# Pooling the first two batches' keys and values on TensorE, with the first weights loaded and decoded ahead of the values

## The chip, the cores and the metric

The kernel runs on one core of a Trainium2 chip. The metric is the time of one execution on the device in microseconds (us), the median over several runs; smaller is better.

## The reference, cut to what matters

Three stages follow each other: attention over pooled keys and values, a dense layer pair with `h * cos(h)` between, and a mixture of eight experts of which each token takes one. The inputs are 8 batches of 8 heads, 576 positions and 64 dimensions, all float32. Only the first stage is touched by the change:

```python
pool = 8
k_p = k.reshape(B, H, Sp, pool, D).mean(axis=3)      # 576 positions -> 72
v_p = v.reshape(B, H, Sp, pool, D).mean(axis=3)
scores = scale * np.matmul(q, k_p.transpose(0, 1, 3, 2))
scores = scores - np.max(scores, axis=-1, keepdims=True)
attn = np.exp(scores)
attn = attn / (np.sum(attn, axis=-1, keepdims=True) + 1e-09)
out = np.matmul(attn, v_p)
# x: 4608 tokens of 512 values
h = x @ w_in;  x = (h * np.cos(h)) @ w_out           # 512 -> 2048 -> 512
```

Each mean is over eight neighbouring positions of one batch; the kernel takes sums and puts the factors 1/8 elsewhere (into the scale of the exponential and into the division of the rows).

## The kernel before, in words

The 4608 tokens are worked in 12 groups (`g`) of 384, and each group in 16 steps (`s`), one for each 128 of the 2048 hidden columns. Step `s` runs `mm1(s)` on TensorE (12 matmuls, L394), `chain_a(s)` and `chain_b(s)` on ScalarE, VectorE and GpSimd (the cosine, L402 to L413), and `mm2(s - 2)` on TensorE (9 matmuls, L420). The attention of group `g + 1` is threaded through the steps of group `g`: `scores` (L335 to L350), `norm` (L355 to L358), `transp` (L365 to L371) and `pv` (L382 to L386). After the 12 groups come the experts.

**Order of the work.** The order is written out by hand: every engine runs its own instructions in the order in which the program issues them, and waits in place when an operand isn't ready. What is issued on SyncE (SP) is DMAs; they too start in program order. A list `ex[s]` holds what is called at the end of step `s` of a group (`at(s, f, ...)` appends to it).

**The weights.** `w_in` and `w_out` lie in memory as 64-bit floats. A pair of pieces `k` (16 pairs, 1 MB each, 512 KB a piece) passes through four functions: `w_load(k)` (two DMAs, L510), `w_scale(k)` (two ScalarE instructions, L514), `w_bits(k)` (six VectorE instructions, L519 to L521; it uses two PSUM banks in between) and `w_parts(k)` (two casts on ScalarE, L526, and two subtractions on GpSimd, L527). In group 0, step `s` calls, inside `chain_a(s)`, `w_bits(s + 3)`, `w_parts(s + 2)`, `w_scale(s + 4)` and `w_load(s + 5)`; `chain_b(s - 1)` is called between the second and the third instruction of `w_bits(s + 3)`. Pairs 0 to 2 are decoded ahead of group 0 (L604 to L622). From group 1 on the weights stay on the chip.

**Pooling.** `load_k` and `load_v` (L307 to L320) bring four tiles of a batch each, 288 KB a tile, the keys as 128 x 576 and the values as 72 x 1024, so that the eight neighbours stand side by side, and `pool_k` and `pool_v` (L313, L324) sum them with one VectorE reduction a tile. Batch 0 is pooled before group 0, with its values between the scores and the first `w_bits`; the keys of batch 1 are pooled at the end of steps 0 and 1 of group 0, its values at the end of step 14. Batches 2 to 7 are pooled in later groups; the change leaves them as they are.

**PSUM banks.** `rot()` hands out banks in turn: seven of them ahead of group 0, and only two (banks 6 and 7) from L625 on. `w_bits`, `scores`, `transp` and `pv` draw from it, so an instruction that writes a bank waits until the former holder's last reader is done.

**Around the start.** After the scores of the first three token tiles, the program before issues on ScalarE in this order: the exponentials of tiles 0 and 1 (L348, eight each), the one of tile 2 (L350), `w_scale(0)`, the copies of transposed tiles 0 and 1 (L369), `w_scale(1)`, the copies of tile 2, `w_parts(0)`, and then the casts of `pv` (L385) with `w_scale(2)` and `w_parts(1)` between.

Of the kernel before, what the change touches and what calls it, by code (L numbers as in the profile page):

```python
# [19 lines left out]
B, H, S, D = 8, 8, 576, 64  # L20
KP = 72
NT = B * S
DM = 512
# [51 lines left out]
    return np.concatenate([p[:, None] < p[None, :], np.ones((128, 128))], axis=1).astype(np.float32)  # L75


@with_exitstack
def attention_moe_kernel(ctx, tc, qT, kT, vP, w_in, w_out, wg, w1, w2, cst, tri, wgt, out, dbg=None):
    nc = tc.nc  # L80
    PE, ACT, DVE, POOL, SP = nc.tensor, nc.scalar, nc.vector, nc.gpsimd, nc.sync

# [37 lines left out]
    def w_tmp(s):  # L120
        n_tmp[0] += 1
        return wbp.tile([128, 1024], F32, name=f"tmp{n_tmp[0]}", tag=f"wb{s}")
# [175 lines left out]
    def raw():  # L298
        kvb_i[0] += 1
        return kvb[kvb_i[0] % len(kvb)]  # L300
# [4 lines left out]
    kraw = {}  # L305

    def load_k(b, c):  # L307
        t = w_tmp(12 + c)[:, 0:S] if b == 0 else raw()[:, 0:S] if b == 1 else kin
        SP.dma_start(out=t, in_=kT[b, c])
        kraw[b, c] = t  # L310

# [3 lines left out]
    vraw = {}  # L315

    def load_v(b, c):
        t = w_tmp(8 + c)[0:KP] if b == 0 else raw()[0:KP]
        SP.dma_start(out=t, in_=vP[b, c])
        vraw[b, c] = t  # L320

    def pool_v(b, c):
        t = vraw.pop((b, c))
        DVE.tensor_reduce(vp[b % 2][:, 128 * c:128 * c + 128], t.rearrange("p (f j) -> p f j", j=8), axis=AX.X, op=ALU.add)  # L324

    def scores(T, i, act=False):
        t0 = i * TP
# [24 lines left out]
    def norm(i, act=False):  # L352
        att, rs = atts[i % len(atts)], rss[:, i]
        if not act:
            DVE.tensor_reduce(rs, att, axis=AX.X, op=ALU.add)  # L355
        DVE.tensor_scalar(rs, rs, 1e-9, 8.0, op0=ALU.add, op1=ALU.mult)
        DVE.reciprocal(rs, rs)
        POOL.tensor_tensor(att, att, rs.unsqueeze(2).to_broadcast([128, H, KP]), op=ALU.mult)  # L358
# [185 lines left out]
    def w_load(k):  # L544
        if k < NCH:
            o = 2 * (k % 3 if k < 11 else (k - 11) % 2)
            for p, t in zip(pairs[k], ring[o:o + 2]):
                p.load(t)

    def w_scale(k):  # L550
        if k < NCH:
            for p in pairs[k]:
                p.scale()
# [11 lines left out]
    def w_parts(k):  # L565
        if k < NCH:
            for p in pairs[k]:
                p.parts()
# [7 lines left out]
    for i in range(3):  # L576
        t = slice(i * TP, i * TP + TP)
        SP.dma_start(out=qs[:, :, t], in_=qT[:, :, t].rearrange("c p t -> p c t"))
    for c in range(4):
        load_v(0, c)  # L580
    w_load(0)
    SP.dma_start(out=E3[:, 0:256], in_=tri)
    w_load(1)
    SP.dma_start(out=tbl.rearrange("(p b r) two -> p b (r two)", p=128, b=2),
# [6 lines left out]
    us += [u[:, DM * i:DM * i + DM] for u in (u14, ldt[0]) for i in range(2)]  # L591
    w_load(2)
    scores(0, 0, True)
    pool_v(0, 0)
    scores(1, 1, True)
    norm(0, True)
    pool_v(0, 1)
    scores(2, 2)
    norm(1, True)
    norm(2)  # L600
    w_scale(0)
    pool_v(0, 2)
    pool_v(0, 3)
    w_bits(0)  # L604
    load_q(1)
    kvb[:] = [w_tmp(8 + i) for i in range(4)]
    for c in range(4):
        load_k(1, c)
    w_load(3)
    transp(0, True)  # L610
    transp(1, True)
    w_scale(1)
    transp(2, True)
    w_parts(0)
    w_bits(1)
    w_load(4)
    pv(0, 0)
# [23 lines left out]
    for g in range(NG):  # L641
# [42 lines left out]
        for b in range(1, B):  # L684
            if g == max(0, b * S // GT - 2):
                if b == 1:
                    at(11, lambda: (kvb.__setitem__(slice(0, None), ring[2:4] + ring[0:2]), kvb_i.__setitem__(0, -1)))
                for c in range(4):
                    if b == 1:
                        at(c // 2, pool_k, b, c)  # L690
                        at(11 + c // 2, load_v, b, c)
                        at(14, pool_v, b, c)
                    else:
                        at(2 + 2 * c, pool_k, b, c)
                        at(2 * c, load_k, b, c)
                if b > 1:
                    for c in range(4):
                        at((7, 10, 12, 14)[c], pool_v, b, c)
                        at((5, 7, 10, 12)[c], load_v, b, c)
# [346 lines left out]
def lay_out(inputs):  # L1046
    ca = np.ascontiguousarray

    def raw(a):
        a = ca(a)  # L1050
        return a.view(np.int64) if a.dtype == np.float64 else a

    q, k, v = inputs["q"], inputs["k"], inputs["v"]
    return {
        "qT": ca(q.transpose(1, 3, 0, 2).reshape(4, 128, NT)),
        "kT": ca(k.transpose(0, 1, 3, 2).reshape(B, 4, 128, S)),
        "vP": ca(v.reshape(B, 4, 2, KP, 8, D).transpose(0, 1, 3, 2, 5, 4).reshape(B, 4, KP, 1024)),
        "w_in": raw(inputs["moe_w_in"]),
        "w_out": raw(inputs["moe_w_out"]),
        "wg": ca(np.pad(inputs["moe2_w_gate"].reshape(4, 128, NE).transpose(1, 0, 2), ((0, 0), (0, 0), (0, 32 - NE)))),  # L1060
        "w1": ca(inputs["moe2_w1"].reshape(NE, 4, 128, 4, 256).transpose(0, 2, 3, 1, 4).reshape(NE, 128, 4096)),
        "w2": ca(inputs["moe2_w2"].reshape(NE, 8, 128, DM).transpose(0, 2, 1, 3).reshape(NE, 128, 4096)),
        "cst": shape_constants(),
        "tri": triangle(),
        "wgt": ca(inputs["moe2_w_gate"].T).reshape(NE * DM),
    }
# [14 lines left out]
```

## Time and profile before

| | us |
|---|---|
| median of 3 runs | 1459.31 |
| lowest and highest of the runs | 1457.72 and 1460.7 |
| the profiled execution, its own time | 1458.9 |
| its span, first to last instruction | 1457.1 |

| engine | busy us | share of the span | instructions |
|---|---|---|---|
| TensorE matmuls (PE) | 1406.2 | 97% | 8295 |
| TensorE weight loads (PEld) | 1219.2 | 84% | 8295 |
| VectorE (DVE) | 878.0 | 60% | 1949 |
| ScalarE (ACT) | 736.3 | 51% | 1353 |
| GpSimd (POOL) | 442.9 | 30% | 421 |

How to read it: all times are microseconds from the start of the span. PE is a matmul, PEld the load of its stationary operand, which overlaps. In a timeline a row is a run of equal instructions: start, time from the first to the last end, engine, source line, operation, output and inputs by the program's names, shapes, and how many; what stands in brackets at the end is the idle time of the engine just before, and whose end released it. "L313" is line 313 of the kernel. A float32 matmul shows as two instructions, one of float32r (L394, L420) as one. PEclk is the granted TensorE clock as a share of 2.4 GHz, so 0.50 is 1.2 GHz.

### The profile page before, as it was taken

The numbers are of one execution on the slowest core, as the hardware profiler recorded it, in microseconds if no ns is written. First come the engines' busy times: TensorE is split into PE (matmuls) and PEld (weight loads), VectorE is DVE, ScalarE is ACT, GpSimd is POOL, SyncE is SP. The second block draws the span as 40 slices with busy tenths as digits, with TensorE's granted clock in tenths as the row PEclk, the third lists the DMA queues.
The fourth block names the chain that finished last, engine by engine and source line by source line (L and its number), as shares of the span: only waits on it lengthen the run. The fifth ranks groups of instructions, "written<-read, shape, count | busy, mean of one in ns | idle before, by whom it ended". The sixth has DMA issues, their size and how long they took to land. (4 is left out here: it accounts for less than half of the span.)

```text
span 1457.1 us, 23304 instructions
## 1 busy us (share of the span) xinstructions
PE 1406.2 (97%) x8295; PEld 1219.2 (84%) x8295; DVE 878.0 (60%) x1949; ACT 736.3 (51%) x1353; POOL 442.9 (30%) x421
## 2 busy tenths in 40 slices
PE   5889999999999999999999999998999999999997
PEld 3778888888888888888888888787787878899997
DVE  7986868685868776686867575853352151134222
ACT  5976656575656565665656565561141141123111
POOL 2663324242423233333333232423141121122212
PEclk9999999999999999999999999999999999999999
DMA  9543112100212100211200002115565344011100
GB/s 301 201 149 110 63 47 63 38 2 22 71 39 63 47 23 22 55 55 39 63 30 23 22 1 82 59 37 211 213 233 210 146 156 157 32 44 42 59 30 32
DMA packets 42692, 119.94 MB, mean 82 GB/s; under 512 B 6179, under 2 KB 22179, under 8 KB 39856
## 3 DMA queue, kind: packets, MB, share of 16 engines
q1 hardware_dynamic: 34624, 99.17, 19.8%
q0 software_dynamic: 7920, 18.97, 3.9%
q8 instruction: 72, 1.18, 0.3%
q14 instruction: 76, 0.62, 0.1%
HBM read 101.55 MB, written 19.66 MB: 83 GB/s over the span
## 5 line engine op out<-in xcount | busy, mean ns | idle before, releaser
L394 PE MATMUL bank<-xh,WI 128*128 128x384 f32 x1536 | 436.5, 345 | 6.5 <-DVE tA L411 4.8
L420 PE MATMUL bank<-wb,gh 128*128 128x512 f32 x1152 | 395.8, 398 | 0.0
L394 PEld LDWEIGHTS bank<-xh,WI 128*128 128x128 f32 x1536 | 284.6, 190 | 19.5 <-DVE tA L411 7.0
L420 PEld LDWEIGHTS bank<-wb,gh 128*128 128x128 f32 x1152 | 217.2, 189 | 53.5 <-issue 5.3
L394 PE MATMUL bank<-xl,WI 128*128 128x384 f32 x768 | 260.9, 340 | 0.2 <-DVE xl L386 0.2
L420 PE MATMUL bank<-wb,gl 128*128 128x512 f32 x576 | 228.3, 396 | 0.3 <-POOL gl L413 0.2
L807 PEld LDWEIGHTS bank<-E,wb 128*128 128x128 f32 x1632 | 208.7, 191 | 20.0 <-issue 7.4
L807 PE MATMUL bank<-E,wb 128*128 128x256 f32 x1632 | 213.9, 283 | 5.3 <-DVE xh L811 2.5
L452 DVE SCALAR_TENSOR_TENSOR E<-x2t,wgb 128x512 bf16<-128x512 f32 x264 | 216.6, 820 | 2.1
L817 PE MATMUL bank<-wb,xh 128*128 128x512 f32 x816 | 209.5, 395 | 0.0
L810 ACT ACTIVATE xh<-bank 128x256 fp32r<-128x256 f32 x136 | 52.2, 384 | 293.8 <-PE bank L807 293.8
L811 DVE SCALAR_TENSOR_TENSOR xh<-bank,xh 128x256 fp32r<-128x256 f32 x136 | 57.5, 424 | 217.3 <-ACTq L995 96.5
L413 POOL TENSOR_TENSOR gl<-tA,gh 128x384 fp32r<-128x384 f32 x96 | 107.7, 1122 | 252.5 <-ACT gh L412 245.9
L413 POOL TENSOR_TENSOR gl<-E,gh 128x384 fp32r<-128x384 f32 x96 | 105.3, 1097 | 260.3 <-ACT gh L412 224.1
L817 PEld LDWEIGHTS bank<-wb,xh 128*128 128x128 f32 x816 | 145.5, 189 | 25.4 <-issue 0.2
L394 PEld LDWEIGHTS bank<-xl,WI 128*128 128x128 f32 x768 | 146.5, 191 | 4.8 <-DVE xl L386 0.5
L196 POOL DMA_INDIRECT E<-x2d,E x44 | 46.1, 1048 | 271.2 <-PE bank L631 256.8
L420 PEld LDWEIGHTS bank<-wb,gl 128*128 128x128 f32 x576 | 108.6, 189 | 18.6 <-POOL gl L413 1.0
L405 DVE SCALAR_TENSOR_TENSOR tA<-bank,tA 128x384 f32<-128x384 f32 x96 | 52.8, 550 | 77.9 <-ACT bank L403 77.9
L405 DVE SCALAR_TENSOR_TENSOR E<-bank,E 128x384 f32<-128x384 f32 x96 | 53.1, 553 | 61.7 <-ACT bank L403 61.6
L406 ACT ACTIVATE E<-E 128x384 f32<-128x384 f32 x96 | 50.4, 525 | 72.3 <-DVE E L405 72.0
L402 ACT ACTIVATE tA<-bank,consts 128x384 f32<-128x384 f32 x96 | 55.1, 574 | 52.0 <-PE bank L394 52.0
(222 smaller groups left out, 1729.2 us busy)
## 6 DMA issues: line engine op xcount, KB each, us to landing
rst<-w SPq DMA_DIRECT2D x12, 2048.0 KB
stg<-w SPq DMA_DIRECT2D x6, 2048.0 KB
x2d<-x2t SPq DMA_DIRECT2D x36, 256.0 KB
early<-qT SPq DMA_DIRECT2D x11, 768.0 KB
E<-kT SPq DMA_DIRECT2D x24, 288.0 KB
E<-vP SPq DMA_DIRECT2D x24, 288.0 KB
wgb<-w_in SPq DMA_DIRECT2D x13, 512.0 KB
wgb<-w_out SPq DMA_DIRECT2D x13, 512.0 KB
```

Source lines behind the costliest of these rows:

```text
L196: POOL.indirect_dma_start(out=xg[i], out_offset=None, in_=x2d[0:n], in_offset=bass.IndirectOffsetOnAxis(ap=column(u, i)[0], axis=0), bound ...
L394: PE.matmul(o, lhsT=a, rhs=x[:, c], start=n == 0, stop=n == 11)
L402: ACT.activation(a, h, AF.Identity, scale=INV2PI, bias=consts[:, C_TP + 1:C_TP + 2])
L405: DVE.scalar_tensor_tensor(a, r, MAGIC, a, op0=ALU.subtract, op1=ALU.subtract)
L406: ACT.activation(a, a, AF.Sin, scale=-TWOPI)
L413: POOL.tensor_tensor(gl[s % 2], a, gh[s % 2].bitcast(F32), op=ALU.subtract)
L420: PE.matmul(ACC[i], lhsT=a[:, sl], rhs=w_tile(s)[:, DM * w:DM * w + DM], start=s == 0 and n == 0, stop=s == NCH - 1 and n == 2)
L452: DVE.scalar_tensor_tensor(junk, x2[i], 1.0, wgb[:, DM * e:DM * e + DM], op0=ALU.mult, op1=ALU.mult, accum_out=lgs[:, i, e:e + 1])
L807: PE.matmul(o, lhsT=w_tile(4 * w + s // 2)[:, f], rhs=x[:, c], start=n == 0, stop=n == 11)
L810: ACT.activation(h, o, AF.Relu)
L811: DVE.scalar_tensor_tensor(l, o, 0.0, h.bitcast(F32), op0=ALU.max, op1=ALU.subtract)
L817: PE.matmul(OP[i], lhsT=a[s % 3][:, 128 * i:128 * i + 128], rhs=w_piece(w, s), start=s == 0 and n == 0, stop=s == 7 and n == 2)
```

## The change

The first batch's values, the second batch's keys and the second batch's values now come from memory in their natural order, positions by 512 head columns (`kvN`, three arrays of 576 x 512), and a constant matrix of zeros and ones (`eig`, 128 x 136) comes with them into `eight`. `load_n` brings one such array in three DMAs (two of 256 positions, one of 64). `sum_v` multiplies five chunks of up to 128 positions into one bank, each by a slice of `eight` of 72 columns as the stationary operand with 512 moving columns, and ScalarE copies the result to `vp`. `sum_k` makes 20 matmuls, each with a 128 x 128 block of the keys as the stationary operand and 16 (at the end 8) moving columns of `eight`, and ScalarE copies the result to `kp`. All operands are float32. In the start, `w_load(0)` is issued ahead of the values, `w_scale(0)` stands between the exponentials of tiles 0 and 1, `w_bits(0)` follows the scores of tile 2 with `norm(1)` inside, `sum_v(0, 0)` stands between `transp(1)` and `w_scale(1)`, and `w_parts(0)` goes ahead of `transp(2)`. In group 0, `sum_k` is called at the end of step 0, the load of the second batch's values at step 12 and their `sum_v` at the end of step 14.

```diff
--- before.py
+++ after.py
@@ -75,8 +75,13 @@
     return np.concatenate([p[:, None] < p[None, :], np.ones((128, 128))], axis=1).astype(np.float32)
 
 
+def eighths():
+    p, f = np.arange(128)[:, None], np.arange(KP + 64)[None, :]
+    return (f - 64 == p // 8).astype(np.float32)
+
+
 @with_exitstack
-def attention_moe_kernel(ctx, tc, qT, kT, vP, w_in, w_out, wg, w1, w2, cst, tri, wgt, out, dbg=None):
+def attention_moe_kernel(ctx, tc, qT, kT, vP, kvN, eig, w_in, w_out, wg, w1, w2, cst, tri, wgt, out, dbg=None):
     nc = tc.nc
     PE, ACT, DVE, POOL, SP = nc.tensor, nc.scalar, nc.vector, nc.gpsimd, nc.sync
 
@@ -305,7 +310,7 @@
     kraw = {}
 
     def load_k(b, c):
-        t = w_tmp(12 + c)[:, 0:S] if b == 0 else raw()[:, 0:S] if b == 1 else kin
+        t = w_tmp(12 + c)[:, 0:S] if b == 0 else kin
         SP.dma_start(out=t, in_=kT[b, c])
         kraw[b, c] = t
 
@@ -315,13 +320,40 @@
     vraw = {}
 
     def load_v(b, c):
-        t = w_tmp(8 + c)[0:KP] if b == 0 else raw()[0:KP]
+        t = raw()[0:KP]
         SP.dma_start(out=t, in_=vP[b, c])
         vraw[b, c] = t
 
     def pool_v(b, c):
         t = vraw.pop((b, c))
         DVE.tensor_reduce(vp[b % 2][:, 128 * c:128 * c + 128], t.rearrange("p (f j) -> p f j", j=8), axis=AX.X, op=ALU.add)
+
+    eight = E3[:, GT:GT + KP + 64]
+    chunks = [(j, min(128, S - 128 * j)) for j in range(-(-S // 128))]
+    nat = {}
+
+    def load_n(x, tiles):
+        nat[x] = [t[:, DM * i:DM * i + DM] for t in tiles for i in range(2)]
+        for j, n in chunks[::2]:
+            if n == 128:
+                SP.dma_start(out=tiles[j // 2].rearrange("p (a f) -> p a f", a=2),
+                             in_=kvN[x, 128 * j:128 * j + 256].rearrange("(a p) f -> p a f", p=128))
+            else:
+                SP.dma_start(out=nat[x][j][0:n], in_=kvN[x, 128 * j:128 * j + n])
+
+    def sum_v(x, b):
+        o = rot()
+        for j, n in chunks:
+            PE.matmul(o[0:KP], lhsT=eight[0:n, 64 - 16 * j:64 - 16 * j + KP], rhs=nat[x][j][0:n], start=j == 0, stop=j == len(chunks) - 1)
+        ACT.copy(vp[b % 2], o[0:KP])
+
+    def sum_k(x, b):
+        o = rot()
+        for c in range(4):
+            for j, n in chunks:
+                k = KP * c + 16 * j
+                PE.matmul(o[:, k:k + n // 8], lhsT=nat[x][j][0:n, 128 * c:128 * c + 128], rhs=eight[0:n, 64:64 + n // 8], start=True, stop=True)
+        ACT.copy(kp[b % 2], o[:, 0:4 * KP].rearrange("p (c k) -> p c k", c=4))
 
     def scores(T, i, act=False):
         t0 = i * TP
@@ -576,9 +608,9 @@
     for i in range(3):
         t = slice(i * TP, i * TP + TP)
         SP.dma_start(out=qs[:, :, t], in_=qT[:, :, t].rearrange("c p t -> p c t"))
-    for c in range(4):
-        load_v(0, c)
     w_load(0)
+    SP.dma_start(out=eight, in_=eig)
+    load_n(0, [w_tmp(8 + c) for c in range(3)])
     SP.dma_start(out=E3[:, 0:256], in_=tri)
     w_load(1)
     SP.dma_start(out=tbl.rearrange("(p b r) two -> p b (r two)", p=128, b=2),
@@ -591,27 +623,21 @@
     us += [u[:, DM * i:DM * i + DM] for u in (u14, ldt[0]) for i in range(2)]
     w_load(2)
     scores(0, 0, True)
-    pool_v(0, 0)
+    w_scale(0)
     scores(1, 1, True)
     norm(0, True)
-    pool_v(0, 1)
     scores(2, 2)
-    norm(1, True)
+    w_bits(0, {3: lambda: norm(1, True)})
     norm(2)
-    w_scale(0)
-    pool_v(0, 2)
-    pool_v(0, 3)
-    w_bits(0)
     load_q(1)
-    kvb[:] = [w_tmp(8 + i) for i in range(4)]
-    for c in range(4):
-        load_k(1, c)
+    load_n(1, [w_tmp(11)] + [w_tmp(8 + c) for c in range(2)])
     w_load(3)
     transp(0, True)
     transp(1, True)
+    sum_v(0, 0)
     w_scale(1)
+    w_parts(0)
     transp(2, True)
-    w_parts(0)
     w_bits(1)
     w_load(4)
     pv(0, 0)
@@ -684,13 +710,11 @@
         for b in range(1, B):
             if g == max(0, b * S // GT - 2):
                 if b == 1:
-                    at(11, lambda: (kvb.__setitem__(slice(0, None), ring[2:4] + ring[0:2]), kvb_i.__setitem__(0, -1)))
+                    at(0, sum_k, 1, b)
+                    at(12, load_n, 2, ring[2:4] + ring[0:1])
+                    at(14, sum_v, 2, b)
                 for c in range(4):
-                    if b == 1:
-                        at(c // 2, pool_k, b, c)
-                        at(11 + c // 2, load_v, b, c)
-                        at(14, pool_v, b, c)
-                    else:
+                    if b > 1:
                         at(2 + 2 * c, pool_k, b, c)
                         at(2 * c, load_k, b, c)
                 if b > 1:
@@ -1055,6 +1079,8 @@
         "qT": ca(q.transpose(1, 3, 0, 2).reshape(4, 128, NT)),
         "kT": ca(k.transpose(0, 1, 3, 2).reshape(B, 4, 128, S)),
         "vP": ca(v.reshape(B, 4, 2, KP, 8, D).transpose(0, 1, 3, 2, 5, 4).reshape(B, 4, KP, 1024)),
+        "kvN": ca(np.stack([x[b].transpose(1, 0, 2).reshape(S, DM) for x, b in ((v, 0), (k, 1), (v, 1))])),
+        "eig": eighths(),
         "w_in": raw(inputs["moe_w_in"]),
         "w_out": raw(inputs["moe_w_out"]),
         "wg": ca(np.pad(inputs["moe2_w_gate"].reshape(4, 128, NE).transpose(1, 0, 2), ((0, 0), (0, 0), (0, 32 - NE)))),
```

## Rows read from the trace of the kernel before

**Rows 1.** Busy time by stretches of the span, columns in the first line.

```profile
core 0: us, PE busy (x) PEld busy (x) DVE busy (x) ACT busy (x) POOL busy (x), PEclk, DMA share, GB/s
...
13.60:39.30 25.70, 17.30 (x68) 10.96 (x66) 24.01 (x47) 19.47 (x57) 10.12 (x10) 1.00 1.02 339
39.30:79.00 39.70, 36.01 (x164) 31.71 (x165) 39.70 (x71) 36.00 (x66) 28.86 (x26) 0.91 0.55 188
...
116.10:127.90 11.80, 10.99 (x70) 8.40 (x70) 8.67 (x13) 7.18 (x13) 3.83 (x4) 1.00 0.46 179
127.90:200.00 72.10, 72.10 (x407) 63.60 (x406) 56.56 (x129) 46.15 (x78) 20.48 (x18) 1.00 0.17 55
```

**Rows 2.** VectorE in the start: group of value reductions (total, mean ns), then timeline.

```profile
L324 DVE TENSOR_REDUCE E<-tmp 72x128 f32<-72x1024 f32 x4 | 4.7, 1187 | 1.0 <-DMA tmp<-vP 1.0
...
22.72 1.27 DVE L519 TENSOR_SCALAR bank<-wgb 128x512 uint32<-128x512 uint32 x2
...
26.46 1.29 DVE L519 TENSOR_SCALAR bank<-wgb 128x512 uint32<-128x512 uint32 x2
...
30.05 0.55 DVE L386 TENSOR_TENSOR xl<-bank,xh 128x384 fp32r<-128x384 f32 x1
```

**Rows 3.** Timeline of ScalarE in the start.

```profile
17.33 0.40 ACT L348 ACTIVATE tmp<-bank,mxs 128x72 f32<-128x72 f32 x1
...
22.74 1.23 ACT L514 ACTIVATE wgb<-wgb 128x512 f32<-128x512 f32 x2
...
27.41 1.14 ACT L526 CAST WI<-x2t 128x512 fp32r<-128x512 f32 x2
```

**Rows 4.** Timeline of TensorE in the start.

```profile
20.30 2.78 PE L365 MATMUL bank<-consts,tmp 128*72 128x128 f32 x12 [1.18 <-POOL tmp L358]
...
26.82 5.39 PE L382 MATMUL bank<-early,E 72*64 72x384 f32 x16
```

**Rows 5.** Float32 matmuls among the experts: timeline, group, and stretch with clock.

```profile
1146.56 7.03 PE L878 MATMUL bank<-rst,xl 128*128 128x512 f32 x16
...
L874 PE MATMUL bank<-xl,rst 128*128 128x128 f32 x64 | 7.3, 275 | 0.0
...
1139.00:1153.00 14.00, 14.00 (x83) 10.34 (x81) 0.75 (x1) 1.19 (x2) 2.95 (x3) 1.00 0.17 59
```

**Rows 6.** Two gaps of TensorE in group 0, and the stretches after them.

```profile
42.83 0.69 PE L394 MATMUL bank<-xh,WI 128*128 128x384 f32 x1 [4.50 <-DVE tA L411]
...
42.80:48.60 5.80, 5.77 (x17) 5.38 (x18) 5.80 (x11) 4.42 (x8) 3.52 (x3) 0.50 0.54 185
...
82.39 0.44 PE L335 MATMUL bank<-E,early 64*128 64x72 f32 x2 [2.25 <-DVE x2t L521]
...
82.80:89.50 6.70, 6.54 (x29) 6.29 (x29) 4.62 (x12) 3.42 (x6) 3.09 (x3) 0.50 0.45 158
```

**Rows 7.** Timeline of VectorE, then ScalarE, steps 0 and 1 of group 0.

```profile
38.06 1.28 DVE L521 SCALAR_TENSOR_TENSOR x2t<-wgb,bank 128x512 uint32<-128x512 uint32 x2
...
39.73 1.40 DVE L313 TENSOR_REDUCE E<-tmp 128x72 f32<-128x576 f32 x2
...
46.87 1.28 DVE L519 TENSOR_SCALAR bank<-tmp 128x512 uint32<-128x512 uint32 x2
...
41.49 0.56 ACT L402 ACTIVATE E<-bank,consts 128x384 f32<-128x384 f32 x1
...
44.27 1.27 ACT L514 ACTIVATE tmp<-tmp 128x512 f32<-128x512 f32 x2
```

**Rows 8.** Timeline at steps 14 and 15 of group 0: TensorE, VectorE, ScalarE.

```profile
116.12 0.44 PE L394 MATMUL bank<-xh,WI 128*128 128x384 f32 x1 [1.05 <-DVE E L411]
...
118.17 0.34 PE L394 MATMUL bank<-xh,WI 128*128 128x384 f32 x1
...
117.05 4.58 DVE L324 TENSOR_REDUCE E<-wgb 72x128 f32<-72x1024 f32 x4
...
118.36 0.56 ACT L369 COPY early<-bank 72x512 f32<-72x512 f32 x1
```

## Prediction, made before the changed kernel was run

> **What bounds the kernel now.** I read first the busy time by stretches, then the timelines of VectorE, ScalarE and TensorE in the start, then TensorE's gaps. From 127.9 us on TensorE is busy in all of 72.10 of 72.10 us [rows 1], and nothing of the change lies there: the change is worth what it moves the start of group 1, at 127.9. Ahead of that VectorE is the full engine: 24.01 of 25.70 us, then 39.70 of 39.70 [rows 1]. TensorE has room in the same stretches, 8.4 and 3.7 us. Just before group 1 it turns: TensorE 10.99 of 11.80 us, VectorE 8.67 [rows 1]. So the change takes work off the full engine in the start, and puts work on the full engine at the end of group 0.
>
> What TensorE's work costs depends on its clock. The clock column prints 1.00 in the start, but the durations there say the lower level, 1.2 GHz: the 16 instructions of `pv` run two side by side, so eight steps in 5.39 us, 0.67 us for 384 columns or 1.75 ns a column [rows 4]; among the experts, at a granted 1.00, a float32 instruction of 512 columns takes 7.03 / 16 = 0.44 us, 0.86 ns a column [rows 5]. That is the factor of two between the levels. I price 0.88 us at the lower one.
>
> **What goes.** VectorE loses the four value reductions of batch 0, 4.7 us [rows 2]; the key reductions of batch 1, 1.40 us at step 0 [rows 7] and as much at step 1, 2.8; and the value reductions of batch 1, 4.58 [rows 8].
>
> **What comes on TensorE.** A float32 matmul is two instructions. `sum_v` is 5 matmuls of 512 moving columns: 10 instructions, 4.4 us at the upper level, 8.8 at the lower, against some 4.6 us on VectorE. `sum_k` is 20 matmuls, 40 instructions, each with a load of 128 x 128 weights for 16 columns. The nearest row has such loads with 128 columns: 64 in 7.3 us, 0.114 each [rows 5], so 4.6 us at the upper level, 9.1 at the lower. From below, if the loads hid wholly, 16 of 512 columns of 0.44 us are 0.014 us, 0.55 in all. I take the weight loads' row, as nothing in `sum_k` is long enough to hide them.
>
> **A, the start.** `sum_v(0, 0)` stands behind `transp(1)` on TensorE, and on ScalarE its copy stands ahead of `w_scale(1)`, `w_parts(0)` and the copies of `transp(2)`. Today tile 1's transposes are eight of the twelve from 20.30, so they end at about 22.15 [rows 4]. After the change a pair of scalings (1.23 us) goes ahead of tile 1's exponentials, which end at some 17.8 today [rows 3], and `norm(1)` comes behind three decode instructions of 0.6 each (six take 26.46 - 22.72 = 3.74 [rows 2]). I put the transposes' end 1.0 later, at 23.2. The sum then runs at the lower level: 23.2 + 8.8 = 32.0. The copy takes 0.56 (the row of the same 72x512 [rows 8]): 32.6. Half of `w_scale(1)` (1.23 [rows 3]): 33.2, when `w_bits(1)` can start. VectorE would have been ready at about 23.0 (26.46 less 4.7, and 1.2 for the later exponentials), so the decode ahead gains 3.4 us and then stands still for ten. On ScalarE follow the other half, 33.8, `w_parts(0)` (1.14 [rows 3]), 34.9, and the first copy of tile 2, 35.5, which releases `pv`: a quarter of 5.39 [rows 4] and a cast like the copy put the first L386 at 37.4, against 30.05 [rows 2]. **A is +7.3 us**; at the upper level 4.4 less, +2.9.
>
> Three things in the start cost nothing. The moved `w_load(0)`: constants, keys and queries are 2.05 MB by their shapes, and with the pair 3.1 MB; at 339 GB/s [rows 1] that is 9.1 us, and ScalarE has its turn for it at about 15.4. The value array and the matrix of ones (1.25 MB) take 3.7 us more, well before 23.2; at half that rate they would be 2.5 us late, which I keep for the range. And SP: two of `load_n(1)`'s DMAs go to places that `sum_v(0, 0)` still reads, so SP stands until 32.0 with `w_load(3)` and `w_load(4)` behind it; 0.66 and 1.05 MB at that rate are 5.0 us, so 37.0, and `w_bits(3)` starts at 35.6 + 7.3 = 42.9. The cover is 6 us.
>
> **B, the keys.** With T the end of `w_bits(3)`, today 39.34 [rows 7]: counting the calls of `rot()`, 23 ahead of group 0, `sum_k` gets the bank that the first piece of `w_bits(3)` used, free at T - 0.6. It stands ahead of `mm1(1)` on TensorE. `mm1(0)` ends about 0.9 us after the last L386, so TensorE idles some 2.2 us before `sum_k`. A gap of 2.25 us was followed by a granted 0.50 for the 6.7 us after 82.8, one of 4.50 by 5.8 us [rows 6]. So 6.7 us at the lower level hold 29 instructions, the other 11 take 1.25: 8.0 us. Then `mm1(1)`, 2.4 us at the upper level (116.12 to 118.51 [rows 8]), then ScalarE's row from L402 to the first half of the pair's scaling that `w_bits(5)` needs, 41.49 to 44.9, 3.4 us [rows 7]: the cast of `chain_b(0)` and `w_scale(5)` stand behind `chain_a(1)`. `w_bits(5)` starts at T - 0.6 + 8.0 + 2.4 + 3.4 = T + 13.2; today at 46.87 [rows 7], T + 7.5. **B is +5.7**, the 2.8 us saved on VectorE lying inside the wait. All at the upper level T + 9.8, +2.3; all at the lower T + 16.7, +9.2; with the loads hidden T + 5.7, -1.8. Afterwards VectorE is full again until the weights end, and the loads follow its releases, so the shift stays.
>
> **C, step 14.** `sum_v(2, 1)` takes the bank of `transp(1)`'s first half, which ScalarE copies at 118.36 to 118.92, behind the sine of step 14 [rows 8]. It stands ahead of `mm1(15)`, today at 116.12 after an idle 1.05 [rows 8]. So TensorE idles from 115.07 to 118.92, 3.85 us, then sums 4.4 at the upper level, and `mm1(15)` starts at 123.3, +7.2. TensorE's idle 0.8 of the stretch after [rows 1] can be won back: +6.4. The gap is longer than the one of 2.25, so I take the lower level for 6.7 us: 7.6 instructions, the other 2.4 at 0.44, 7.75 in all. **C is +9.7**; with `mm1(15)` low too, +13.2. The 4.58 us that leave VectorE gain nothing: TensorE worked through them.
>
> **Sum.** 7.3 + 5.7 + 9.7 = 22.7 on the profiled execution's 1458.9 (span 1457.1 and 1.8 around it): 1481.6; the median is 0.4 higher, so 1482.
>
> **Rivals.** *The clock rises during the sums.* Against it: `pv`, 5.39 us without a break, stayed low [rows 4]. For it: the experts' float32 stretch, 14 us, kept 1.00 [rows 5]. All three at the upper level: 2.9 + 2.3 + 6.4 = 11.6, 1470.5. The Trainium skill (TensorE: Matmul & The Clock Gate, Part 1) says that sustained matmul work releases the throttle; by that rule the long unbroken sum would rise, and the total would be nearer 1470 than 1482. The `pv` row speaks against it.
>
> *Faster: VectorE's relief counts.* VectorE is full, and the reductions of the start are 7.5 us: 1451.4. This needs the sums to fit TensorE's idle time. It is decided at `w_scale(1)`: the sum would have to be copied by 22.4, but the transposes ahead of it end at 23.2. And `sum_k` would have to end within 1.8 us of T - 0.6, when VectorE comes to its bank in `w_bits(4)`. Only if ScalarE or TensorE did not keep the written order would both hold.
>
> *No change.* The two early sums hide and the third does not: -7.5 + 6.4, 1457.8.
>
> **Chances.** The forecast 0.63 (its own range 1474 to 1490), the high clock 0.25, faster 0.07, no change 0.05. The range takes in all three sums low (1458.9 + 29.7 = 1488.6) and, below, the high clock with `sum_k`'s loads hidden (1466.4): 1466 to 1490. Within 0.2%, 2.9 us, is about what a measurement can't tell from no change. So faster 0.07, the same 0.05, slower 0.88.
>
> **What would show it.** In the changed profile `sum_v(0, 0)` takes 8 to 9 us from about 23, ScalarE's next scaling comes right behind its copy, and VectorE stands idle for some ten us before the second pair's first L519. VectorE waits for ScalarE's copy in `w_bits(4)`. Before `sum_v(2, 1)` TensorE idles near four us, released by L369. Group 1's first L394 comes at about 150. I am wrong if VectorE runs through from the first decode to the second, or if the sums show under 5 us each.

## The result and the profile after

The changed kernel takes 1476.49 us in the median (1475.44 to 1477.29, four runs) against 1459.17 us (1457.72 to 1460.7, four runs) for the kernel before in the same comparison: a ratio of 1.0115, 95% interval 1.0102 to 1.0127. It is slower by 17.3 us. The forecast was 1482, range 1466 to 1490. In the table, the spans are of the profiled executions, and a piece's cost is how much later the named event comes than before, less what came before it.

| part | event | before | after | cost | forecast |
|---|---|---|---|---|---|
| A, start | end of `w_bits(3)` | 39.34 [rows 7] | 42.52 | +3.2 | +7.3 |
| B, keys | start of `w_bits(5)` | 46.87 [rows 7] | 57.06 | +10.2 in all, +7.0 | +5.7 |
| C, step 14 | start of group 1 | 127.93 | 145.96 | +18.0 in all, +7.8 | +9.7 |
| the rest | span | 1457.1 | 1473.7 | +16.6 in all, -1.4 | 0 |

The first `mm1` of group 1 in the timelines of TensorE, before and after:

```profile
127.93 0.44 PE L394 MATMUL bank<-xh,WI 128*128 128x384 f32 x1
...
145.96 0.44 PE L426 MATMUL bank<-xh,WI 128*128 128x384 f32 x1
```

The page of the changed kernel, its span and the busy times of the engines:

```profile
span 1473.7 us, 23420 instructions
...
PE 1421.9 (96%) x8355; PEld 1225.7 (83%) x8355; DVE 868.2 (59%) x1937; ACT 737.0 (50%) x1356; POOL 441.5 (30%) x421
```

TensorE has 60 instructions and 15.7 us more than in the table of before, VectorE 9.8 us less. The added busy time is close to the added time, and so one rival to the explanation by waits is that the sums simply cost their length. The experiments set these two against each other.

Busy time of the changed kernel by stretches (columns as in [rows 1]):

```profile
core 0: us, PE busy (x) PEld busy (x) DVE busy (x) ACT busy (x) POOL busy (x), PEclk, DMA share, GB/s
13.60:39.30 25.70, 18.46 (x61) 9.53 (x60) 16.58 (x34) 16.53 (x51) 7.72 (x7) 0.83 0.91 284
39.30:79.00 39.70, 37.76 (x173) 32.96 (x173) 30.42 (x54) 30.01 (x56) 22.93 (x22) 0.85 0.48 158
...
22.50:27.70 5.20, 5.20 (x12) 1.41 (x11) 0.00 (x0) 0.58 (x1) 1.07 (x1) 1.00 1.01 306
31.00:36.40 5.40, 5.38 (x17) 1.78 (x17) 4.86 (x9) 2.88 (x6) 1.55 (x2) 0.50 0.94 325
44.40:54.40 10.00, 10.00 (x37) 9.85 (x38) 3.54 (x6) 2.46 (x5) 0.56 (x1) 0.50 0.22 80
129.80:132.80 3.00, 3.00 (x4) 0.77 (x4) 0.00 (x0) 0.00 (x0) 0.00 (x0) 0.50 0.00 0
```

VectorE, full before (24.01 of 25.70 and 39.70 of 39.70 [rows 1]), is now busy for 16.58 and 30.42 us of the same two stretches. Of these 16.7 us, at most 7.5 are the reductions that have left (4.7 and 2.8); the rest is standing still. In the 5.2 us of the first sum VectorE does nothing at all.

The start of the changed kernel, timelines of VectorE, TensorE and ScalarE:

```profile
28.94 1.29 DVE L551 TENSOR_SCALAR bank<-wgb 128x512 uint32<-128x512 uint32 x2 [6.66 <-ACT wgb L546]
...
33.13 0.56 DVE L418 TENSOR_TENSOR xl<-bank,xh 128x384 fp32r<-128x384 f32 x1 [0.52 <-ACT xh L417]
...
22.46 5.26 PE L347 MATMUL bank<-tmp,E 128*72 128x512 f32 x10
...
31.02 5.39 PE L414 MATMUL bank<-early,E 72*64 72x384 f32 x16 [2.29 <-ACT early L401]
...
27.77 0.58 ACT L348 COPY E<-bank 72x512 f32<-72x512 f32 x1 [4.47 <-PE bank L347]
28.25 1.22 ACT L546 ACTIVATE wgb<-wgb 128x512 f32<-128x512 f32 x2
```

The chain of the forecast is all there. ScalarE stands for 4.47 us before the copy of the sum, the scaling of the second pair follows directly, and VectorE has waited 6.66 us for that scaling. The sum, though, took 5.26 us and not 8.8.

The keys in the changed kernel, timelines of TensorE, VectorE and ScalarE around step 1:

```profile
41.25 1.27 DVE L553 SCALAR_TENSOR_TENSOR x2t<-wgb,bank 128x512 uint32<-128x512 uint32 x2
...
41.98 7.58 PE L355 MATMUL bank<-E,tmp 128*128 128x16 f32 x40 [1.44 <-DVE x2t L553]
...
50.03 0.69 DVE L551 TENSOR_SCALAR bank<-wgb 128x512 uint32<-128x512 uint32 x1 [5.82 <-ACT E L356]
...
57.06 1.29 DVE L551 TENSOR_SCALAR bank<-tmp 128x512 uint32<-128x512 uint32 x2 [1.43 <-ACT tmp L546]
...
53.78 0.58 ACT L434 ACTIVATE E<-bank,consts 128x384 f32<-128x384 f32 x1 [3.79 <-PE bank L426]
```

The first row is the last of `w_bits(3)`, which ends at 42.52. `sum_k` waits for the bank of `w_bits(3)`; VectorE waits 5.82 us for the copy of the sum in `w_bits(4)`; ScalarE waits 3.79 us for `mm1(1)`, which stood behind the sum.

Step 14 of the changed kernel, timelines of TensorE, ScalarE and VectorE:

```profile
129.12 6.36 PE L347 MATMUL bank<-wgb,E 128*72 128x512 f32 x10 [4.59 <-ACT early L401]
135.40 0.44 PE L426 MATMUL bank<-xh,WI 128*128 128x384 f32 x1
...
128.50 0.56 ACT L401 COPY early<-bank 72x512 f32<-72x512 f32 x1
...
138.74 0.69 DVE L403 COPY early<-bank 72x512 f32<-72x512 f32 x1 [11.47 <-PE bank L397]
```

TensorE idles 4.59 us until ScalarE has copied the bank (128.50 + 0.56), sums for 6.36 us, and only then starts `mm1(15)`. VectorE, relieved of 4.58 us of reductions [rows 8], is without work for 11.47 us.

The last 1.4 us come back late: near 936 us the kernel before has a TensorE gap of 2.14 us and then a granted 0.50 for 3.4 us; the changed kernel has the same gap (2.13 us, at 953.7) and a granted 1.00 after it. Nothing of the change lies there.

### The profile page after: what moved, and what is told of

It is laid out like the page before. It is cut to its first block, busy times and chain, and to the rows that moved or that the text cites. A ratio compares the mean times of both kernels' runs of the same rounds, so it can differ in the third digit from the quotient of the medians.

```text
span 1473.7 us, 23420 instructions
## 1 busy us (share of the span) xinstructions
PE 1421.9 (96%) x8355; PEld 1225.7 (83%) x8355; DVE 868.2 (59%) x1937; ACT 737.0 (50%) x1356; POOL 441.5 (30%) x421
## 5 line engine op out<-in xcount | busy, mean ns | idle before, releaser
L426 PEld LDWEIGHTS bank<-xh,WI 128*128 128x128 f32 x1536 | 283.4, 190 | 17.3 <-DVE E L443 4.5
L444 ACT CAST gh<-E 128x384 fp32r<-128x384 f32 x96 | 49.3, 514 | 62.9 <-DVE E L443 62.2
```

The lines of the kernel that those rows point to most:

```text
L426: PE.matmul(o, lhsT=a, rhs=x[:, c], start=n == 0, stop=n == 11)
L444: ACT.copy(gh[s % 2], a)
```

## The experiments

Two theories. **Written order**: a sum costs what stands waiting behind it on the in-order engines, so the same sum in another place costs little. **TensorE's work**: a sum costs its length on TensorE wherever it stands. All kernels compute the whole reference. They ran on four chips (13: x1, x2, x4, x5; 15: x0, x3, x6, x7; 14: x8, x9; 4: x10, b0), the kernel before each time on the same chip (medians there 1466.36, 1465.8, 1466.96 and 1459.45 us), and the ratios are to that. The record doesn't name the chip of the first comparison. The changed kernel ran again on chip 15 alone, so the runs on chip 13 are held against its ratios, not against a run beside them. Two anchors from each trace stand beside the ratio: the time from the first instruction of `w_bits(3)` to that of `w_bits(6)`, in which B lies, and the start of group 1. The kernel before itself differs by 0.5 and 1.1 us in these two between its traces, so differences below that say little.

| run | `w_bits(3)` | to `w_bits(6)` | group 1 | ratio, 95% interval |
|---|---|---|---|---|
| before, first trace | 35.7 | 15.7 | 127.9 | 1 |
| changed, first trace | 38.9 | 22.7 | 146.0 | 1.0115 (1.0102 to 1.0127) |
| x0_changed_again | 39.7 | 24.0 | 146.0 | 1.0129 (1.0103 to 1.0156) |
| x1_v1_vector | 39.0 | 24.3 | 139.7 | 1.0070 (1.0053 to 1.0087) |
| x2_k_vector | 40.2 | 16.2 | 140.0 | 1.0079 (1.0062 to 1.0096) |
| x3_v0_vector | 36.2 | 26.3 | 146.8 | 1.0120 (1.0103 to 1.0137) |
| x4_v1_step15 | 39.7 | 24.1 | 144.6 | 1.0113 (1.0095 to 1.0130) |
| x5_k_own_bank | 40.1 | 16.6 | 140.8 | 1.0073 (1.0056 to 1.0090) |
| x6_v0_after_copies | 39.8 | 24.3 | 149.8 | 1.0133 (1.0116 to 1.0150) |
| x7_v0_early | 34.7 | 15.7 | 128.0 | 0.9991 (0.9981 to 1.0000) |
| x8_v0_own_bank | 34.1 | 15.7 | 126.0 | 0.9999 (0.9986 to 1.0011) |
| x9_v0_and_k | 33.9 | 15.8 | 125.1 | 1.0015 (1.0002 to 1.0027) |
| x10_all_moved | 33.8 | 15.8 | 129.4 | 1.0042 (1.0027 to 1.0056) |
| b0_before_again | 35.6 | 16.3 | 129.0 | 1.0000 (0.9990 to 1.0009) |

### The changed kernel again

No edit.

> The changed kernel unchanged, as the common yardstick on this chip. Both theories expect the ratio measured before, 1.010 to 1.013, and the three sums where they were: the first at 22.5 us for 5.3 us with ScalarE's copy right behind it and VectorE idle for 6 to 7 us.

Ratio 1.0129. The first sum took 6.41 us here and VectorE waited 7.82 us for the scaling behind its copy, both longer than expected; the third, at a granted 1.00, shows what C is without a low clock:

```profile
130.90 4.66 PE L347 MATMUL bank<-wgb,E 128*72 128x512 f32 x10 [3.85 <-ACT early L401]
```

The idle time is the 3.85 us of the forecast. From the first instruction of `mm1(14)` to group 1 it is 24.3 us here and 18.2 and 19.0 in the two traces of the kernel before: C is +5.3 to +6.2 by this measure, below the forecast's all-upper +6.4. By the events of the table, against the first trace of before, this run has A +4.1, B +8.2 (the keys took 8.82 us) and C +5.8: again 18.1 in all, split otherwise.

### Undoing one part: C, B, A

C undone: the values of batch 1 are reduced on VectorE again.

```diff
-                    at(12, load_n, 2, ring[2:4] + ring[0:1])
-                    at(14, sum_v, 2, b)
+                    at(11, lambda: (kvb.__setitem__(slice(0, None), ring[2:4] + ring[0:2]), kvb_i.__setitem__(0, -1)))
...
+                        at(11 + c // 2, load_v, b, c)
+                        at(14, pool_v, b, c)
```

> The second batch's values go back to VectorE (loads at steps 11 and 12, four reductions at step 14); all else as in the changed kernel (1476.5 us). Theory of the written order: a sum costs what stands waiting behind it. In the changed profile group 1 starts 18.0 us later than before, and 10.1 us of that were there at step 13, so this part is 7.9 us: about 1468.6. Rival, TensorE's work: its busy time grew by 15.7 us (1406.2 to 1421.9), almost the whole difference, and each sum costs its length there: 6.4 us, about 1470.1. This run gives the size of the part; the next one tells the theories apart.

Ratio 1.0070, and from `mm1(14)` to group 1 19.0 us. The part that C added is gone: the kernel before has 18.2 and 19.0 there.

B undone: the keys of batch 1 are reduced on VectorE again, at steps 0 and 1.

```diff
-                    at(0, sum_k, 1, b)
...
+                        at(c // 2, pool_k, b, c)
```

> The second batch's keys go back to VectorE (four loads in the start, two reductions each at the ends of steps 0 and 1); all else as in the changed kernel. Written order: in the changed profile w_bits(5) starts 10.2 us later than before and w_bits(3) ended 3.2 later, so this part is 7.0 us: about 1469.5. TensorE's work: the 7.6 us of the 40 instructions, about 1468.9. For the size; the next run tells them apart.

Ratio 1.0079, and from `w_bits(3)` to `w_bits(6)` 16.2 us, as in the kernel before (15.7 and 16.3), instead of the 24.1 and 24.3 of the two runs on this chip that keep the sum in its place.

A undone but for the early decode: the values of batch 0 are reduced on VectorE, behind `norm(2)`.

```diff
-    load_n(0, [w_tmp(8 + c) for c in range(3)])
+    for c in range(4):
+        load_v(0, c)
...
     norm(2)
     load_q(1)
+    for c in range(4):
+        pool_v(0, c)
...
-    sum_v(0, 0)
```

> Values of batch 0 back on VectorE, right behind norm(2), with the early decode kept; the other two sums stay. Written order: VectorE's wait of 6.66 us before the second pair is replaced by 4.7 us of reductions, so w_bits(1) starts at about 27.0 instead of 28.9 and the time falls by some 2 us against the changed kernel, no more (VectorE is full again). TensorE's work: ten instructions leave TensorE, so it falls by the 5.3 us that they took.

`w_bits(3)` starts 3.5 us earlier than in the changed kernel on this chip, so A is gone there (`w_bits(1)` starts at 27.02, as expected), but the ratio is 1.0120: neither theory's gain arrives. ScalarE, then TensorE, in the timeline of this run:

```profile
34.97 0.70 ACT L546 ACTIVATE wgb<-wgb 128x512 f32<-128x512 f32 x1 [1.68 <-DMA wgb<-w_in]
37.80 0.65 ACT L546 ACTIVATE wgb<-wgb 128x512 f32<-128x512 f32 x1 [2.13 <-DMA wgb<-w_out]
...
41.05 9.43 PE L355 MATMUL bank<-E,tmp 128*128 128x16 f32 x40 [4.27 <-DVE x2t L553]
```

The load of the fourth pair is what comes late next, 3.8 us of waits in all. And since TensorE had finished `mm1(0)` earlier, its gap before `sum_k` grew to 4.27 us, and the 40 instructions ran at a granted 0.50 throughout, 0.24 us each. Of the 3.5 us that A gave back, B took 2.3 (26.3 against 24.0 us); the third sum took more than the rest, 6.36 us with a stretch at a granted 0.50 against 4.66 in the changed kernel on this chip.

### Moving a sum instead of undoing it

C moved: the same sum one step later, behind `mm1(15)`.

```diff
-                    at(14, sum_v, 2, b)
+                    at(15, sum_v, 2, b)
```

> The sum of the second batch's values stays on TensorE but is called at the end of step 15 instead of step 14, so mm1(15) no longer stands behind it. Written order: the idle 4.59 us ahead of the sum goes and the clock stays at 2.4 GHz, so the sum takes about 4.4 us; mm1(15) can start at 126.2 of the changed profile, 11.0 us of its later work and 4.4 of the sum follow, so group 1 starts near 142 instead of 146.0: 4 us less, about 1472.5. TensorE's work: the same ten instructions still run, so nothing, or at most the 2 us by which the higher clock shortens them: 1474.5 to 1476.5.

The sum, in this run's timeline of TensorE, has no idle time ahead of it, and what follows waits 0.20 us:

```profile
134.08 4.60 PE L347 MATMUL bank<-wgb,E 128*72 128x512 f32 x10
...
139.35 1.52 PE L414 MATMUL bank<-early,E 72*64 72x192 f32 x14 [0.20 <-ACT E L348]
```

From `mm1(14)` to group 1 it takes 22.8 us: 4.6 more than before, which is the sum's length, and 1.6 to 4.1 less than with the sum in step 14 (24.3 and 26.9). So of C the wait is the part that order makes, and the length stays, because TensorE is the full engine there. The whole time, 1.0113, shows no gain that stands clear of the changed kernel's interval, and the 4 us that written order expected did not come. By the time alone this run is inconclusive.

B moved: the same 40 instructions, into a bank of the accumulators that is free until step 2, and behind `mm1(1)`.

```diff
-        o = rot()
+        o = ACC[2]
...
-                    at(0, sum_k, 1, b)
+                    at(1, sum_k, 1, b)
```

> The sum of the keys stays on TensorE, but writes an accumulator bank that is unused until step 2 and is called at the end of step 1, so it stands behind mm1(1) and waits for no bank of the decode. Written order: it runs in TensorE's gap between mm1(1) and mm1(2) (4.5 us in the profile before); nothing of VectorE waits for it and 2.8 us of reductions stay saved: between 7.0 and 9.8 us less, 1466.7 to 1469.5. TensorE's work: the same 40 instructions, no change, 1476.5.

```profile
42.97 6.27 PE L355 MATMUL bank<-E,tmp 128*128 128x16 f32 x40
...
53.47 0.58 ACT L434 ACTIVATE tA<-bank,consts 128x384 f32<-128x384 f32 x1 [2.70 <-PE bank L426]
```

In the timelines of TensorE and ScalarE the sum still takes 6.27 us, but nothing waits for its bank; ScalarE waits 2.70 us for `mm1(2)`, which stands behind it. B shrinks to 16.6 us from `w_bits(3)` to `w_bits(6)`, near the 16.2 without the sum on the same chip. The ratio, 1.0073, is that of undoing B, just short of what was expected. This is the first clear result against TensorE's work: the same instructions, six us and more cheaper in this stretch. Part of that gain is the clock, since the sum took 7.58 to 9.44 us in its old place and `mm1(1)` behind it 3.9 to 4.2 us, 2.3 us here. But the clock does not explain that a sum of 6.27 us now costs 0.4 us, net of the 2.8 us that VectorE is spared.

A moved behind `transp(2)`, so that ScalarE's scaling is not held:

```diff
-    sum_v(0, 0)
     w_scale(1)
     w_parts(0)
     transp(2, True)
+    sum_v(0, 0)
```

> The same sum of batch 0's values behind transp(2), so that w_scale(1) and w_parts(0) are no longer held by its copy; TensorE's work is the same. Written order: w_bits(1) starts at about 24.5 instead of 28.9, but pv still stands behind the sum's copy, so its first VectorE subtraction moves from 33.1 to about 32 and the time falls by some 1 us; if only VectorE's wait had counted, by 3.2. TensorE's work: no change (0).

The second pair's decode starts at 24.89 us, as early as expected, and the ratio is 1.0133, unchanged. ScalarE, VectorE and TensorE in its timelines say why:

```profile
31.98 0.58 ACT L348 COPY E<-bank 72x512 f32<-72x512 f32 x1 [4.58 <-PE bank L347]
...
34.04 0.56 DVE L418 TENSOR_TENSOR xl<-bank,xh 128x384 fp32r<-128x384 f32 x1 [5.49 <-ACT xh L417]
...
32.62 2.80 PE L414 MATMUL bank<-early,E 72*64 72x384 f32 x16 [0.67 <-ACT E L348]
```

The wait of VectorE for the scaling (7.82 us on this chip) shrank to 1.60 us, and 5.49 us came back in front of the first subtraction of `pv`. The expected 1 us did not come either: that subtraction stands at 34.04, against 34.06 in the changed kernel on this chip. One wait was traded for another.

### The sums where nothing full stands behind them

Batch 0's values alone on TensorE, ahead of the transposes, where it idled, with the scalings of the second and third pair moved up; keys and values of batch 1 on VectorE as in the two undoings above.

```diff
     norm(2)
+    w_scale(1)
+    sum_v(0, 0)
     load_q(1)
...
-    sum_v(0, 0)
-    w_scale(1)
...
-    pv(0, 0)
     w_scale(2)
+    pv(0, 0)
```

> Keys and values of batch 1 back on VectorE; the sum of batch 0's values stays on TensorE but ahead of the transposes, where TensorE idles after the scores (13.7 to 17 us), w_scale(1) stands ahead of the copies and w_scale(2) ahead of the first pv cast. Written order: nothing full waits for the sum any more; w_bits(1) starts at about 22.5 (26.5 in the kernel before), w_bits(3) at 32 to 33.5 (35.7), and the time falls below the kernel before by 1 to 4 us, ratio 0.997 to 0.9995. TensorE's work: the ten instructions still cost their 5.3 us, ratio 1.0035.

TensorE, then VectorE, in the start of this run:

```profile
15.52 7.37 PE L347 MATMUL bank<-tmp,E 128*72 128x512 f32 x10 [1.58 <-ACT att L380]
...
27.09 2.80 PE L414 MATMUL bank<-early,E 72*64 72x384 f32 x16 [1.46 <-ACT early L401]
...
23.54 1.29 DVE L551 TENSOR_SCALAR bank<-wgb 128x512 uint32<-128x512 uint32 x2 [0.99 <-ACT E L348]
```

The sum takes 7.37 us, longer than in the changed kernel, and the kernel is no slower than the one before: ratio 0.9991, where the sum's length would have made 1.0035 or more. This is the net of the sum, of the 4.7 us of reductions that left VectorE and of the scalings that were moved; the run doesn't tell them apart. `w_bits(3)` starts at 34.7, 1.0 us before that of the kernel before, short of the 32 to 33.5 expected.

The same with a bank of its own and the casts of the first pair behind `transp(2)`:

```diff
-        o = rot()
+        o = RB
...
-    w_parts(0)
     transp(2, True)
+    w_parts(0)
```

> Only the sum of batch 0's values on TensorE, ahead of the transposes as in the run before, but into a bank that nothing else uses until the cosine of step 0, and w_parts(0) behind the copies of transp(2). Written order: the 0.99 us that the second pair's decode waited for the sum's copy and about 1 us of the 1.87 us wait for the first pv cast go; w_bits(3) starts at 33 to 34 (34.7 in the run before, 35.7 in the kernel before) and the ratio is 0.997 to 0.999. If the loads of pair 3 end last instead (their scaling started at 32.3 and ended at 33.0), w_bits(3) stays at 34 and more and the ratio is 0.999 to 1.000. TensorE's work: 1.0035.

The 0.99 us wait is gone and the decode starts at 22.77, but `w_bits(3)` only at 34.1. In ScalarE's timeline the scaling of the fourth pair waits for both its loads:

```profile
32.19 0.69 ACT L546 ACTIVATE wgb<-wgb 128x512 f32<-128x512 f32 x1 [1.53 <-DMA wgb<-w_in]
...
33.44 0.67 ACT L546 ACTIVATE wgb<-wgb 128x512 f32<-128x512 f32 x1 [0.56 <-DMA wgb<-w_out]
```

That is the second case that had been named: the loads of the weights end last, and the time stays at 0.9999. Group 1 starts 1.9 and 3.0 us earlier than in the two traces of before; the time does not show it.

With the keys on TensorE as well, in the accumulators' bank behind `mm1(1)`:

```diff
-                        at(c // 2, pool_k, b, c)
+                    if b == 1 and c == 0:
+                        at(1, sum_k, 1, b)
```

> The same with the keys on TensorE too, in their own bank and behind mm1(1). Written order: no wait of a full engine is added by order alone, but TensorE has only 2.9 us idle ahead of mm1(2) here where the keys took 6.3 us before, so they push mm1(2) by some 3 us while VectorE is relieved of 2.8 us: about even with the run without them, minus 1 to plus 2 us, ratio 0.997 to 1.001. TensorE's work: their 6.3 us on top, ratio 1.004 to 1.008.

Busy time by stretches, one row of the run before and one of this run, then the sum in TensorE's timeline and a row of ScalarE's:

```profile
39.30:79.00 39.70, 37.06 (x168) 31.02 (x168) 39.48 (x71) 36.24 (x68) 28.62 (x25) 0.96 0.57 195
39.30:79.00 39.70, 39.12 (x192) 34.47 (x192) 37.18 (x66) 36.29 (x70) 28.36 (x24) 0.96 0.56 190
...
37.25 5.21 PE L355 MATMUL bank<-E,tmp 128*128 128x16 f32 x40
...
46.39 0.58 ACT L434 ACTIVATE tA<-bank,consts 128x384 f32<-128x384 f32 x1 [1.81 <-PE bank L426]
```

No engine waits for the sum's bank, and yet from `w_bits(3)` to `w_bits(6)` it is 15.8 us, the 15.7 of the run without it: the 2.8 us that left VectorE gained nothing. `mm1(2)` stands behind the sum and ScalarE waits 1.81 us for it, 0.39 in the run before; VectorE then waits 1.49 us for ScalarE's scaling in front of `w_bits(6)`. TensorE is now busy for 39.12 of 39.70 us, against 37.06, and VectorE for 37.18, against 39.48: TensorE has become the fuller engine. The ratio is 1.0015, just above what written order expected and above the run without the keys, though the two intervals overlap and group 1 starts 0.9 us earlier; the part behind 962 us took 504.0 us in this trace and 500.8 in the other, and why is open.

All three sums on TensorE, the same 60 instructions as in the changed kernel, each in its better place:

```diff
+                        at(12, load_n, 2, ring[2:4] + ring[0:1])
+                        at(15, sum_v, 2, b)
...
-        o = RB
+        o = RB if x == 0 else rot()
```

> All three sums on TensorE, with the same 60 instructions as in the changed kernel, but each where nothing full stands behind it: batch 0's values ahead of the transposes in their own bank, the keys behind mm1(1) in their own bank, batch 1's values at the end of step 15. Written order: the first two cost nothing (group 1 started at 125.1 us without the third), the third its own length on a full TensorE, 4.4 to 4.7 us; group 1 starts at 129 to 131 (127.9 before, 146.0 changed) and the ratio is 1.001 to 1.005. TensorE's work: the sums cost their length wherever they stand, so the ratio stays at 1.010 to 1.013.

The third sum and the start of group 1 in TensorE's timeline:

```profile
118.94 4.60 PE L347 MATMUL bank<-wgb,E 128*72 128x512 f32 x10
...
129.45 0.44 PE L426 MATMUL bank<-xh,WI 128*128 128x384 f32 x1
```

Group 1 starts at 129.4, 4.4 us later than without the third sum, which takes 4.60 us. The ratio is 1.0042, within what written order expected and far below 1.010. So about two thirds of the loss of the changed kernel come from the places of the sums, together with the scalings and casts of the start that moved with them. What the rest is, no trace shows. The profiled execution, 1458.86 us at a mean granted clock of 0.996, lies at the low end of this kernel's times (up to 1469.76 us, at 0.987; median 1464.65), and in it group 1 starts only 0.5 us later, and the last `mm1` ends 1.2 us earlier, than in the trace of the kernel before on the same chip. The 5 us by which the medians differ lie in executions at a lower clock, of which there is no trace.

### The kernel before again

No edit.

> The kernel before itself, for a trace of it on this chip; both theories expect a ratio of 1.000 within its interval. What it is to tell: whether its last mm1 ends near 965 us with about 500 us of experts behind it (497 to 504 in the experiments here, 492 in the first trace), which would say that the 7 us between the chips lie among the experts and not in the part that the change touches.

The ratio is 1.0000. The last `mm1` ends at 966.0 and 492.0 us follow, as in the first trace (492.1). But this was a chip on which the kernel before takes 1459 us, not one of those with 1466, so it only narrows the question: `x10_all_moved` on the same chip has 492.2 us there, and the kernels on the other three 497 to 504. No trace of the kernel before was taken on those.

## Why the prediction was right, and where its terms were off

**The direction and the mechanism were right.** VectorE was the full engine and was relieved, and its relief was worth nothing, because each sum put a wait into an in-order queue in front of it. The waits are those that were named: ScalarE's scaling behind the copy of the first sum, VectorE in `w_bits(4)` behind the copy of the keys, `mm1(15)` behind a bank that ScalarE copies. The range held the time; the forecast was 5.5 us too high: A was 4.1 us and C 1.9 too high, B 1.3 too low, and 1.4 us came back behind group 1. Two of the signs that it named did not show: the first sum took 5.26 us and not 8 to 9, and VectorE stood idle for 6.66 us and not some ten.

**A was mis-sized, +3.2 instead of +7.3.** The step that failed is "The sum then runs at the lower level: 23.2 + 8.8 = 32.0". It ran for 5.26 us, 6.41 in the second run of the same kernel, and 5.28 to 7.37 in the other kernels. In no trace did it take 8.8. The price of an instruction was nearly right (4.60 to 4.66 us for ten in three traces at the upper level, 4.4 forecast); the error was to take the neighbour, `pv`, as evidence for the level. `pv` itself again took 5.39 us, now printed with a granted 0.50 from 31.0 on. The rival's +2.9 for A was nearly exact, in part by luck: the sum ended at 27.7 us, where the rival would have it at 27.6, but it started 0.7 us earlier than that and took 0.9 longer. The Trainium skill (TensorE: Matmul & The Clock Gate, Part 1) has activity release the throttle; the first sum agrees, with 5.26 us, and that had been the rival's ground; `pv`, at the lower level for 5.39 us without a break, does not. The rest was as forecast: the transposes ended at 22.67 (23.2), the copy took 0.58 (0.56), the scaling came directly behind it.

**B was +7.0 instead of +5.7.** The sum started 0.54 us before the end of `w_bits(3)` (0.6 forecast) and took 7.58 us (8.0), near by luck: the lower level was forecast for its beginning and came from 44.4 on, 2.4 us into it; in the second run it took 8.82. The failed step is "Then `mm1(1)`, 2.4 us at the upper level": a granted 0.50 lasted past the sum, and `mm1(1)` took 4.2 us, from 49.49 until ScalarE could go on at 53.78. A low level after a gap was foreseen, but it was given 6.7 us from the rows of two other gaps, and here the stretch from 44.4 to 54.4 was low.

**C was +7.8 instead of +9.7.** The wait was right (4.59 and 3.85 us measured, 3.85 forecast), the sum's length again was taken too long: 6.36 us, 3 of them at a granted 0.50, and 4.66 us, against 7.75. The second run gives +5.8 by the same events, less than the forecast's upper-level value of +6.4. Between the two runs the sum's length, and with it the clock, differs by 1.7 us and the wait by 0.7.

**The start's loads were no cost, and they were a limit.** In the changed kernel the fourth pair's scaling waits for no load, as was forecast. The forecast did not ask what a faster start would meet; the experiments did: at 32 to 34 us the loads of that pair end last, which caps what a relief of VectorE in the start can bring. Whether an earlier issue of these loads would lift the cap was not tested.

**The rivals.** *Faster* fails twice: in the changed kernel by the waits, and with the waits taken away by the load of the fourth pair and by TensorE, which has little room for the keys (39.12 of 39.70 us busy with them). *The clock rises* was right for the first sum, wrong for the keys, and half right for the third; the time, 1476.5, lies halfway between it and the forecast. *TensorE's work*, set up after the result, is refuted as a rule by the moved sums (1.0042 with the same instructions, 0.9991 with one of them). It holds at step 15, where TensorE is full: there the sum added about its 4.60 us to the start of group 1.

**A version that beats both?** None was found. The best, batch 0's values alone on TensorE in its idle time, has the ratio 0.9991, with an interval up to 1.0000. Against the changed kernel on the same chip its median is 1.2% lower (1464.69 against 1482.8). The moved scalings without any sum on TensorE were not tried, so how much of this is the sum's stays open.

## What to carry to other kernels

Moving work from a full engine to one with room pays only if nothing full stands behind it in the queue of the new engine, in the queue of the engine that copies its result, or at the buffer that it borrows. Price the place, not only the length: the kernel with the same 60 instructions on TensorE is 1.2% slower in one order and 0.4% in another. And before hoping for the saved time, ask what ends last once the full engine is faster; here it was a load of weights in the start and, with the keys on it, TensorE after that.

## What was not expected of the hardware

**A neighbour's clock is no price.** In the kernel before, `pv` ran for 5.39 us at the lower level without a break [rows 4]; in the kernels with the first sum, its ten float32 instructions of 512 columns, ahead of `pv`, rose to the upper level within their run. `pv` then took 2.80 us in the five kernels in which TensorE idled for at most 1.46 us ahead of it, 4.69 to 5.39 in the two runs of the changed kernel and the four that keep its start, where 2.3 us of idle time lay between, and 5.39 in the kernel without the first sum (x3_v0_vector). So `pv` was at the upper level throughout only behind a sum that had risen, and only with little idle time between; why the sum rises and `pv` alone doesn't stays open.

**The clock column misled.** It prints 1.00 for `pv` in the kernel before and 0.50 in the changed one, and the duration is 5.39 us in both. In the second trace of the kernel before, where `pv` takes 5.17 us, the column says 0.53 for just that stretch. The duration of a known instruction was the better witness.

**Small float32 matmuls cost as much as ones of 128 columns.** 40 instructions with 16 moving columns took 5.21 us at a granted 1.00, 0.13 us each, and 9.43 us, 0.24 each, in a run with no rise: near the 0.114 and 0.23 taken in the prediction from the rows with 128 columns, and far from the 0.014 of hidden loads.

**The last stage varies more than the change in the start.** The same instructions behind the last `mm1` took 492 us in the four traces of the first comparison and of the last chip, and 497 to 504 in the ten on the three others; the changed kernel itself has 492.5 in one trace and 497.2 in another. That the chip makes this is likely and not shown. A gain of 2 us ahead of it, as in the two runs with group 1 at 125 and 126 us, does not show in a time there.
